# Attention and gated feed-forward on one core: softmax totals on VectorE, layer-norm sums on ScalarE, and a new order

## Chip, core and metric

The kernel runs on one core of one Trainium2 chip. The metric is the device time of one execution in microseconds (us). The engines are TensorE (PE, matmuls; PEld are its weight loads), VectorE (DVE), ScalarE (ACT), GpSimd (POOL) and SyncE (SP, which here only starts DMA transfers). Every engine works through its own instruction list in order and waits, where it must, on semaphores of the others.

## What is computed

The input x has 2048 rows of 512 bf16 numbers. It is normalized row by row; the result xn feeds an attention with 32 heads of 16 numbers, in which every row looks at itself and 7 earlier rows at distances 2, 4, ..., 14, and a gated feed-forward of width 1792:

```python
xn = _layernorm(x)                                  # (x - mean) / sqrt(var + 1e-5)
q, k, v = split(xn @ wqkv)                          # 32 heads x 16
logits = einsum("bhsd,bhswd->bhsw", q, kg) * scale  # kg: the 8 keys at s, s-2, ..., s-14
attn = softmax(where(mask, logits, -1e9))
s = einsum("bhsw,bhswd->bhsd", attn, vg) @ wo
h = gelu(xn @ w_gate) * (xn @ w_up)
return x + s * silu(h @ w_down)
```

## The kernel before

The rows are worked on in four blocks of 512 (j = 0 to 3), each of four tiles of 128 rows. In each block:

- **Layer norm** (`layernorm`, L211; `first_tile`, L321). Per tile, DVE takes the statistics (`stats`, L219, and `aggr`, L223: mean and variance into `mv`). In block 0 ACT takes a square root and DVE inverts it and normalizes; PE transposes the result and ACT copies it into xT. In blocks 1 to 3, POOL computes 1/sqrt(variance + eps) for four tiles at once (`power`, L239 to 243: an addition and a power), DVE makes -mean times that (`shift`, L234, tile `nmr`), ACT normalizes (`norm_act`, L256) and four DMA transposes on SP's queue (`cross`, L307) make xT.
- **q, k, v** (`qkv`, L378; in block 0 `qkv_tiles`, L463, tile by tile). PE multiplies, ACT copies out of PSUM to q, k and a staging tile vst. v goes through DRAM: POOL's queue stores vst to vT (L434; block 0 L497) and loads it back in another layout with the rows that the window reaches back to (`v_loads`, L522, four loads per block, L529). In block 0 the first load needs the first store only.
- **Scores** (`scores`, L542). DVE multiplies q by shifted k (L562, in block 0 half of the products in two halves) and adds the four column groups (L578, two levels); PE adds up within each head with a 0/1 matrix (`reduce`, L600, into the PSUM tile L). DVE takes the maximum over the window (`peak`, L617) and subtracts it (`less`, L624), ACT takes exp (L631), PE adds up the 8 weights with an identity matrix (`total`, L635, 8 matmuls into L), DVE inverts (`recip`, L642) and multiplies (`share`, L646).
- **Values** (`values`, L665). DVE multiplies weights by v (L670, 8 products) and adds them as a tree (L678) to o.
- **Feed-forward** (`ffn`, L701). 14 column groups: PE computes gate and up (L712), ACT evaluates gelu (L728) and copies up (L736), DVE multiplies two groups at a time ("geglu", L750) into h. `down` (L757): PE multiplies h by w_down (L773) in four pieces per tile, of 4, 4, 4 and 2 matmuls; a piece needs the geglu products of its groups. ACT takes silu (L788).
- **Output** (`out`, L799). PE projects o with wo (L807, 64 matmuls into four PSUM tiles), ACT copies out (L821), DVE multiplies by the silu and adds x (L832 and L836; in block 3 per tile, L857 and L863), SP stores.

PSUM: pool F has 6 slots for all these products, of which the projection takes four at once; pool L has one.

The order of every engine's list is not written out. Each operation is entered with an engine, a planned duration, what it needs and a priority (`op`, L167); the function `schedule` (L69) plays this plan through once while the program is built and emits the operations in the order in which they would have started. Its planned durations, latencies (`LAT`), DMA constants (L44 and 45), due times per block (`PARAMS`, L50: N for the layer norm, S scores, V values, Q q/k/v, F feed-forward, Y down) and a seeded jitter of priorities decide the order; none of them changes an instruction. The loads at the start (`loads`, L882) are issued by SP one after the other: x of block 0, wq, wk, wv, x of block 1, gate and up weights, x of block 2, w_down, x of block 3, wo (four copies of it).

Of the kernel before, what the change touches and what calls it, by code (L numbers as in the profile page):

```python
# [41 lines left out]
LAT = {"PE": 0.2, "DVE": 0.1, "ACT": 0.13, "POOL": 0.15}  # L42
DEPENDENT = 0.115
DMA_FIXED = 2.3  # L44
DMA_RATE = {"SP": 325e3, "POOL": 180e3}

POOLS = {"F": 6, "L": 1, "q": 2, "k": 2, "pr": 8, "attn": 2, "Ls": 1, "v": 2, "o": 1, "h": 1,
         "xT": 2, "gl": 3, "sil": 1, "s16": 1, "xn": 4, "vst": 4}

PARAMS = dict(  # L50
    ladd=2, ln_act=4, warm=4, slack=1.0, jitter=(1899, 1.0), N=[-18.9, 13.0, 103.0, 122.5],
    S=[43.3, 66.6, 104.1, 114.9], V=[-8.5, 67.0, 115.5, 125.8], Q=[-7.2, 61.3, 75.8, 119.6],
    F=[3.3, 63.6, 104.7, 160.7], Y=[50.2, 87.1, 133.4, 194.0],
)


# [12 lines left out]
def schedule(ops, pools):  # L69
# [26 lines left out]
    while any(ready.values()):  # L96
        best = None
        for e, rs in ready.items():
            if not rs:
                continue  # L100
            ests = []
            for o in rs:
                t = max(clock[e], at[o.name])
                ok = True
                if o.take:
                    p, n = o.take[0][0], len(o.take)
                    ok = len(free[p]) >= n
# [12 lines left out]
        if best is None:  # L120
            raise RuntimeError("stuck: " + str({e: [o.name for o in r][:6] for e, r in ready.items()}))
        t, o = best
        e = o.eng
        ready[e].remove(o)
        for p, b in o.take:
            _, slot[b] = heapq.heappop(free[p])
        o.start = t
        if o.bytes:
            clock[e] = t + o.dur
            wire[e] = max(wire[e], t + o.dur / 2) + o.bytes / DMA_RATE[e]  # L130
            end = wire[e] + DMA_FIXED
            lanes[e][lane[e]] = end
            lane[e] = (lane[e] + 1) % 8
        else:
            if o.table and o.table != table:
                t += TABLE
                table = o.table
            clock[e] = t + o.dur
            end = clock[e] + LAT[e]
        o.done = end if o.bytes else clock[e] + (DEPENDENT if e == "DVE" else 0.0)  # L140
        o.end = end
        order.append(o)
        for b in o.use:
# [15 lines left out]
class Kernel:  # L159
# [51 lines left out]
    def layernorm(self, j):  # L211
        base = self.when("N", j)
        for tt in range(TPB):
# [25 lines left out]
            def power(a, b):  # L239
                nc = self.nc  # L240
                r = self.rstd[:, a:b, 0]
                nc.gpsimd.tensor_scalar(out=r, in0=self.mv[:, a:b, 1], scalar1=EPS, scalar2=None, op0=ALU.add)
                nc.gpsimd.tensor_tensor(out=r, in0=r, in1=self.mhalf[:, 0 : b - a], op=ALU.pow)

            def norm_dve(t=t):
                nc = self.nc
# [29 lines left out]
            if t == 0:  # L276
                self.first_tile()
                continue
            self.op(f"stats{t}", "DVE", 0.69, [f"ld_x{t if j == 0 else j}_{j}"] + {1: ["aggr0"], 2: ["copy1"]}.get(t, []),
                    stats, prio=prio, slack=(0.0, 0.5, 3.0, 3.0)[j])  # L280
            self.op(f"aggr{t}", "DVE", 0.16, [f"stats{t}"], aggr, prio=prio)
            on_act = t >= self.par["ln_act"]
            if j == 0:
                self.op(f"root{t}", "ACT", 0.25, [f"aggr{t}"], root, prio=prio, table="sqrt")
                self.op(f"rstd{t}", "DVE", 0.1, [f"root{t}"], inverse, prio=prio)
                if on_act:
                    self.op(f"shift{t}", "DVE", 0.1, [f"rstd{t}"], lambda f=shift, t=t: f(t, t + 1), prio=prio)
                ready = f"shift{t}" if on_act else f"rstd{t}"
            else:
                a, b = j * TPB, (j + 1) * TPB  # L290
                if tt == 0:
                    self.op(f"rstd{j}_", "POOL", 1.4, [f"aggr{i}" for i in range(a, b)],
                            lambda f=power, a=a, b=b: f(a, b), prio=prio)
                    self.op(f"shift{j}_", "DVE", 0.1, [f"rstd{j}_"], lambda f=shift, a=a, b=b: f(a, b), prio=prio)
                ready = f"shift{j}_"
            if on_act:
                self.op(f"norm{t}", "ACT", 0.75, [ready], norm_act, take=[("xn", f"xn{t}")],
                        use=[f"xn{t}"], prio=prio)
# [243 lines left out]
    def scores(self, j):  # L542
# [87 lines left out]
            at = self.new(f"at{j}", [P, W, P], BF16, "attn")  # L630
            self.nc.scalar.activation(out=at[:], in_=self.t[f"Ls{j}"][:], func=AF.Exp)  # L631

        def total(j=j):
            for w in range(W):
                self.nc.tensor.matmul(  # L635
                    self.t[f"L{j}"][:, 0, 0:P], lhsT=self.ident[:], rhs=self.t[f"at{j}"][:, w, :],
                    start=(w == 0), stop=(w == W - 1),
                )

        def recip(j=j):  # L640
            with self.nc.allow_low_precision(reason="the weights that it scales are bf16"):
                self.nc.vector.reciprocal(out=self.rs[:, j % 2, :], in_=self.t[f"L{j}"][:, 0, 0:P])  # L642

        def share(j=j):
            at = self.t[f"at{j}"]
# [6 lines left out]
        if j == 0:  # L652
# [3 lines left out]
                use=[f"L{j}", f"Ls{j}"], prio=hot)  # L656
        self.op(f"expo{j}", "ACT", 0.95, [f"less{j}"], expo, take=[("attn", f"at{j}")],
                use=[f"Ls{j}", f"at{j}"], prio=-10.0, table="exp")
        self.op(f"total{j}", "PE", W * MM128, [f"expo{j}"], total, use=[f"at{j}", f"L{j}"], prio=-100.0,
                slack=self.par["slack"])  # L660
        self.op(f"recip{j}", "DVE", 0.95, [f"total{j}"], recip, use=[f"L{j}"], prio=hot)
        self.op(f"share{j}", "DVE", 0.6, [f"recip{j}"], share, use=[f"at{j}"], prio=hot)


# [217 lines left out]
    def loads(self, src):  # L882
# [33 lines left out]
        half = NF // 2 * P  # L916
        kb = 1024
        xt = [(f"ld_x{t}_0", lambda t=t: x_tile(t), 128 * kb) for t in range(TPB)]
        x0 = [("ld_x0_0a", lambda: x_tile(0, 0, D // 2), 32 * kb),
              ("ld_x0_0b", lambda: x_tile(0, D // 2, D, "scalar"), 32 * kb),  # L920
              ("ld_x1_0", lambda: x_tile(1), 192 * kb)]
# [27 lines left out]
def kernel(  # L949
# [33 lines left out]
    k.mhalf = cpool.tile([P, TPB], F32, name="mhalf")  # L983
    k.nmr = cpool.tile([P, NT, 1], F32, name="nmr")
    k.peak = cpool.tile([P, 2, P], F32, name="peak")
    k.rs = cpool.tile([P, 2, P], BF16, name="rs")
    k.ident = cpool.tile([P, P], BF16, name="ident")
    k.ind = cpool.tile([P, H], BF16, name="ind")
# [58 lines left out]
```

## Time and profile before

| what | value |
|---|---|
| time, median of 3 runs | 219.7 us (219.17 to 220.0) |
| time of the profiled execution | 219.26 us |
| its span | 217.3 us |
| last matmul ends | 213.87 us |
| DVE waits for ACT at the last block's output | 5.4 us, once |
| ACT waits for PE at silu (L788) | 21.5 us in 11 waits |
| ACT table loads | 17, of 1.283 us each |
| DMA: v loads (L529), median to landing | 3.8 us; the longest 15.2 us |
| DMA: wo, four copies, median to landing | 16.4 us |

How to read it: the profile shows one execution. Busy times of an engine are the times of its instructions; matmuls are pipelined, so that their durations overlap and the distance from one start to the next tells the pace. The timeline gives start, length and, in brackets, how long the engine was idle before and who ended that. A group line gives the source line, the engine, the operation, its tiles and shapes, the count, then busy us and mean ns of one, then idle time ahead of it. On ACT and DVE an independent instruction starts some 0.1 us before the one ahead of it has ended by the record, so spacing is shorter than length: whole products on DVE are 1.22 us long and 1.135 us apart.

### The profile page before, as it was taken

To read this page: it belongs to the slowest core of one execution; us is meant where nothing else is said; L and a number is where in the kernel's file an instruction comes from. 1 tells how busy PE (TensorE), PEld (TensorE's weight loads), DVE (VectorE), ACT (ScalarE), POOL (GpSimd) and SP (SyncE) were. 2 spreads that over 40 slices of the span, in tenths; PEclk is the share of its full clock that TensorE was granted. 3 is DMA by queue.
4 is the path that set the end of the run, shared out by engine and by line. 5 is a ranking of instruction groups with operands and counts; after the bars stand their busy time and mean duration, and the time that the engine had idled before them with its cause. 6 is when DMAs were issued, how large, how long until landed. Compare 5 with 4: busy or idle time off the path is not lost.

```text
span 217.3 us, 3417 instructions
## 1 busy us (share of the span) xinstructions
PE 209.9 (97%) x1346; PEld 103.1 (47%) x1366; DVE 191.3 (88%) x229; ACT 145.2 (67%) x238; POOL 27.0 (12%) x59
## 2 busy tenths in 40 slices
PE   7999998999999999999999999999999999999993
PEld 2996443444544444454444434544444454444452
DVE  4685999999999997899999969599999999999433
ACT  3687984898987477797624757976732795866151
POOL 5025220220001114002320000001150000000000
PEclk9999999999999999999999999999999999999999
DMA  5999999994000118000490000200123000011002
GB/s 165 363 384 371 306 313 195 187 128 75 0 0 3 48 48 206 0 0 24 112 166 2 0 5 0 97 2 0 53 81 75 0 0 3 0 37 62 0 24 72
DMA packets 18671, 19.59 MB, mean 90 GB/s; under 512 B 7632, under 2 KB 17504, under 8 KB 18528
## 3 DMA queue, kind: packets, MB, share of 16 engines
q1 hardware_dynamic: 16688, 14.88, 26.4%
q0 software_dynamic: 1824, 4.44, 8.1%
q8 instruction: 10, 0.16, 0.3%
q10 hardware_dynamic: 144, 0.07, 0.1%
q14 instruction: 5, 0.04, 0.1%
HBM read 13.60 MB, written 4.21 MB: 82 GB/s over the span
## 4 chain that ended last, share of the span: by engine, by line
PE 70%; DVE 22%; DMA 4%; issue 1%; POOL 1%; ACT 0%; DVEq 0%; POOLq 0%
PE y_ps L773 17%; PE u_ps L712 16%; PE g_ps L712 16%; PE qkv_ps L392 10%; DVE prod L562 7%; PE s_ps L807 7%; DVE prod L578 6%; DVE pv L670 3%; DMA vT_dram<-vst 3%; PE qkv_ps L473 2%; DVE hT L750 2%; DVE pv L678 2%; DMA x_sb<-in_A_x_dram 1%; PE L_ps L600 1%; PE L_ps L635 1%
## 5 line engine op out<-in xcount | busy, mean ns | idle before, releaser
L712 PE MATMUL g_ps<-xnT,wg_sb 128*128 128x512 bf16 x219 | 55.3, 379 | 0.3
L712 PE MATMUL u_ps<-xnT,wu_sb 128*128 128x512 bf16 x219 | 54.8, 379 | 0.2
L773 PE MATMUL y_ps<-wd_sb,hT 128*128 128x512 bf16 (+2 forms) x233 | 49.1, 366 | 0.4 <-issue 0.2
L562 DVE TENSOR_TENSOR prod<-q_sb,k_sb 128x2048 bf16<-128x2048 bf16 (+1 forms) x36 | 38.5, 1101 | 1.6 <-ACT k_sb L489 1.0
L736 ACT ACTIVATE hT<-u_ps 128x512 bf16<-128x512 f32 x56 | 32.9, 600 | 9.5 <-PE u_ps L712 8.7
L728 ACT ACTIVATE gl<-g_ps 128x512 bf16<-128x512 f32 x56 | 33.2, 604 | 7.8 <-PE g_ps L712 7.6
L670 DVE TENSOR_TENSOR pv<-attn,v_arr 128x2048 bf16<-128x2048 bf16 x32 | 38.1, 1220 | 0.1
L773 PEld LDWEIGHTS <-hT 128*128 128x128 bf16 x238 | 22.9, 98 | 25.7 <-issue 0.8
L712 PEld LDWEIGHTS <-wg_sb 128*128 128x128 bf16 x224 | 21.8, 98 | 26.3 <-issue 0.4
L712 PEld LDWEIGHTS <-wu_sb 128*128 128x128 bf16 x224 | 21.5, 98 | 26.4 <-issue 1.5
L678 DVE TENSOR_TENSOR pv<-pv 128x2048 bf16<-128x2048 bf16 x24 | 29.2, 1220 | 0.1
L578 DVE TENSOR_TENSOR prod<-prod 128x2048 bf16<-128x2048 bf16 x24 | 29.1, 1218 | 0.1
L788 ACT ACTIVATE sil<-y_ps 128x512 bf16<-128x512 f32 (+2 forms) x17 | 9.6, 573 | 21.6 <-PE y_ps L773 21.5
L750 DVE TENSOR_TENSOR hT<-hT,gl 128x1024 bf16<-128x1024 bf16 x28 | 19.1, 687 | 2.6 <-ACT hT L736 2.3
L434 POOL DMA_DIRECT2D vT_dram<-vst x12 | 6.7, 559 | 96.2 <-ACT vst L414 96.0
L821 ACT ACTIVATE s<-s_ps 128x512 bf16<-128x512 f32 x16 | 8.9, 602 | 14.4 <-PE s_ps L807 14.4
L807 PE MATMUL s_ps<-wo_sb,o_sb 32*128 32x512 bf16 x256 | 14.5, 375 | 0.0
L529 POOL DMA_DIRECT2D v_arr<-vT_dram x16 | 10.5, 661 | 16.4 <-DMA vT_dram<-vst 12.0
L392 PE MATMUL qkv_ps<-xnT,wk_sb 128*128 128x512 bf16 x46 | 11.9, 380 | 0.1
L392 PE MATMUL qkv_ps<-xnT,wv_sb 128*128 128x512 bf16 x48 | 11.8, 379 | 0.0
L392 PE MATMUL qkv_ps<-xnT,wq_sb 128*128 128x512 bf16 x45 | 11.5, 379 | 0.0
L256 ACT ACTIVATE xn<-x_sb,nmr,rstd 128x512 bf16<-128x512 bf16 x12 | 9.5, 815 | 2.2 <-DVE nmr L234 1.1
(77 smaller groups left out, 177.4 us busy)
## 6 DMA issues: line engine op xcount, KB each, us to landing
v_arr<-vT_dram POOLq DMA_DIRECT2D x16, 142.0 KB, 3.8
vT_dram<-vst POOLq DMA_DIRECT2D x16, 128.0 KB, 2.1
wo_sb<-in_A_wo_dram SPq DMA_DIRECT2D x4, 512.0 KB, 16.4
wg_sb<-in_B_w_gate_dram SPq DMA_DIRECT2D x2, 896.0 KB, 11.0
wu_sb<-in_B_w_up_dram SPq DMA_DIRECT2D x2, 896.0 KB, 13.1
wd_sb<-in_B_w_down_dram SPq DMA_DIRECT2D x1, 1792.0 KB, 19.7
x_sb<-in_A_x_dram SPq DMA_DIRECT2D x3, 512.0 KB, 15.4
out_dram<-s SPq DMA_DIRECT2D x3, 512.0 KB, 3.0
```

Of the source, the lines that this page charges most:

```text
L392: self.nc.tensor.matmul(ps[:], lhsT=self.w_qkv(which, dk, c), rhs=self.t[f"xT{j}"][:, dk, :], start=(dk == 0), stop=(dk == NC - 1),)
L529: self.nc.gpsimd.dma_start(out=self.t[f"v{j}"][H * tq : H * (tq + 1), :, :], in_=self.vT.rearrange("(h d) s -> h d s", d=DH)[:, :, a : a + ...
L562: nc.vector.tensor_tensor(out=self.t[f"pr{j}_{w2}_{c}"][:, :, a:b], in0=self.t[f"q{j}"][:, c, a:b].unsqueeze(1).to_broadcast([P, 4, b - a] ...
L578: self.nc.vector.tensor_tensor(out=pa[:], in0=pa[:], in1=pb[:], op=ALU.add)
L670: self.nc.vector.tensor_tensor(out=pv[:], in0=self.t[f"at{j}"][:, w, :].unsqueeze(1).to_broadcast([P, DH, P]), in1=self.t[f"v{j}"][:, :, 2 ...
L678: self.nc.vector.tensor_tensor(out=out[:], in0=pa[:], in1=pb[:], op=ALU.add)
L712: nc.tensor.matmul(ps[:], lhsT=w[:, dk, fc * P : (fc + 1) * P], rhs=self.t[f"xT{j}"][:, dk, :], start=(dk == 0), stop=(dk == NC - 1),)
L728: self.nc.scalar.activation(out=self.t[f"gl{j}_{pair}"][:, fc % 2, :], in_=self.t[f"ps_g{j}_{fc}"][:], func=AF.Gelu_apprx_tanh,)
L736: self.nc.scalar.activation(out=self.t[f"h{j}"][:, fc, :], in_=self.t[f"ps_u{j}_{fc}"][:], func=AF.Copy)
L750: self.nc.vector.tensor_tensor(out=h, in0=h, in1=self.t[f"gl{j}_{pair}"][:], op=ALU.mult)
L773: nc.tensor.matmul(self.t["ps_" + key][:, 0 : n1 - n0], lhsT=self.t[f"h{j}"][:, fc, tt * P : (tt + 1) * P], rhs=self.wd_sb[:, fc, n0:n1], ...
L807: nc.tensor.matmul(self.t[f"ps_s{j}_{tq}"][:], lhsT=self.t[f"o{j}"][r, d, :], rhs=self.wo_sb[r, d, :], start=(d == 0), stop=(d == DH - 1),)
```

## The change

Three things, and an order that the plan makes anew from them:

1. The totals of the softmax weights are added up on DVE, 8 weights to 4, to 2, to 1, in an fp32 tile `tot` in SBUF, in place of 8 matmuls per block; the reciprocal reads that tile in place of PSUM.
2. In blocks 1 to 3 ACT takes the layer-norm sums with its accumulator: one pass over the tile scaled by -1/512 gives the negative mean, a second one (the square, with that mean as bias) the sum of squared deviations. The full outputs of both go to a scratch tile `junk`. POOL scales the sum by 1/512, adds eps, takes the power and also multiplies the negative mean by it (what DVE's `shift` did).
3. The plan gives a DMA on POOL's queue 3.5 us more to land when it starts before 42 us, and counts other sizes for the first x loads. Due times, slack and jitter seed are others.

```diff
+DMA_CROWDED = 3.5
+LOADED = 42.0
...
-    ladd=2, ln_act=4, warm=4, slack=1.0, jitter=(1899, 1.0), N=[-18.9, 13.0, 103.0, 122.5],
-    S=[43.3, 66.6, 104.1, 114.9], V=[-8.5, 67.0, 115.5, 125.8], Q=[-7.2, 61.3, 75.8, 119.6],
-    F=[3.3, 63.6, 104.7, 160.7], Y=[50.2, 87.1, 133.4, 194.0],
+    ladd=2, ln_act=4, warm=4, slack=0.43, jitter=(4125, 1.0), N=[-7.6, 3.9, 71.2, 106.4],
+    S=[59.8, 41.3, 100.0, 71.3], V=[4.5, 66.8, 111.5, 104.5], Q=[-0.7, 60.2, 73.9, 128.3],
+    F=[10.2, 64.4, 112.5, 164.8], Y=[33.1, 91.5, 146.3, 187.2],
...
-            end = wire[e] + DMA_FIXED
+            end = wire[e] + DMA_FIXED + (DMA_CROWDED if e == "POOL" and t < LOADED else 0.0)
...
-                nc.gpsimd.tensor_scalar(out=r, in0=self.mv[:, a:b, 1], scalar1=EPS, scalar2=None, op0=ALU.add)
+                nc.gpsimd.tensor_scalar(
+                    out=r, in0=self.mv[:, a:b, 1], scalar1=1.0 / D, scalar2=EPS, op0=ALU.mult, op1=ALU.add
+                )
                 nc.gpsimd.tensor_tensor(out=r, in0=r, in1=self.mhalf[:, 0 : b - a], op=ALU.pow)
+                nc.gpsimd.tensor_tensor(out=self.nmr[:, a:b, 0], in0=self.mv[:, a:b, 0], in1=r, op=ALU.mult)
...
+            if j:
+
+                def mean(t=t):
+                    self.nc.scalar.activation(
+                        out=self.junk[:], in_=self.x_sb[:, t, :], func=AF.Identity, scale=-1.0 / D,
+                        accum_out=self.mv[:, t, 0:1],
+                    )
+
+                def square(t=t):
+                    self.nc.scalar.activation(
+                        out=self.junk[:], in_=self.x_sb[:, t, :], func=AF.Square, bias=self.mv[:, t, 0:1],
+                        accum_out=self.mv[:, t, 1:2],
+                    )
+
+                self.op(f"mean{t}", "ACT", 0.65, [f"ld_x{j}_{j}"], mean, prio=prio, slack=(0.0, 0.5, 3.0, 3.0)[j])
+                self.op(f"aggr{t}", "ACT", 0.65, [f"mean{t}"], square, prio=prio)
+            else:
+                self.op(f"stats{t}", "DVE", 0.61, [f"ld_x{t}_0"] + {1: ["aggr0"], 2: ["copy1"]}.get(t, []),
+                        stats, prio=prio)
+                self.op(f"aggr{t}", "DVE", 0.16, [f"stats{t}"], aggr, prio=prio)
...
-                    self.op(f"shift{j}_", "DVE", 0.1, [f"rstd{j}_"], lambda f=shift, a=a, b=b: f(a, b), prio=prio)
-                ready = f"shift{j}_"
+                ready = f"rstd{j}_"
...
-        def total(j=j):
-            for w in range(W):
-                self.nc.tensor.matmul(
-                    self.t[f"L{j}"][:, 0, 0:P], lhsT=self.ident[:], rhs=self.t[f"at{j}"][:, w, :],
-                    start=(w == 0), stop=(w == W - 1),
-                )
+        def total(i, j=j):
+            half = W >> (i + 1)
+            t = self.tot
+            src = t if i else self.t[f"at{j}"]
+            self.nc.vector.tensor_tensor(
+                out=t[:, 0:half, :], in0=src[:, 0:half, :], in1=src[:, half : 2 * half, :], op=ALU.add
+            )
...
-                self.nc.vector.reciprocal(out=self.rs[:, j % 2, :], in_=self.t[f"L{j}"][:, 0, 0:P])
+                self.nc.vector.reciprocal(out=self.rs[:, j % 2, :], in_=self.tot[:, 0, :])
...
-        self.op(f"total{j}", "PE", W * MM128, [f"expo{j}"], total, use=[f"at{j}", f"L{j}"], prio=-100.0,
-                slack=self.par["slack"])
-        self.op(f"recip{j}", "DVE", 0.95, [f"total{j}"], recip, use=[f"L{j}"], prio=hot)
+        last = f"expo{j}"
+        for i in range(3):
+            last = self.op(f"total{j}_{i}", "DVE", (0.6, 0.33, 0.2)[i], [last], lambda i=i, f=total: f(i),
+                           use=[f"at{j}"], prio=hot)
+        self.op(f"recip{j}", "DVE", 0.95, [last], recip, prio=hot)
...
+    k.junk = cpool.tile([P, D], BF16, name="junk")
+    k.tot = cpool.tile([P, W // 2, P], F32, name="tot")
```

What the new order moves, read from the built programs: on POOL the rstd of block 1 and its two companions stand behind the four v stores of block 0 and the first v load, and ahead of the other three v loads (before, they stood behind two stores and the first load; two stores and three loads followed). On ACT the 24 new passes stand between the copies and gelus of block 0 and the first half of block 1, all ahead of the copies of the output projection of block 0. On PE the projection of block 2 moves behind the feed-forward of block 3, the reduction of block 3 into the down products of block 2, and the projections of blocks 0, 1 and 3 stand a few matmul groups earlier. SP issues the same transfers in the same order. ACT loads its tables 17 times, as before.

More of the change, by code (lines that the diff above doesn't have):

```diff
@@ L278, in layernorm @@
                 continue
[L279 to L282, printed above, removed]
+            if j:
[15 more added lines that the diff above has]
+                self.op(f"aggr{t}", "DVE", 0.16, [f"stats{t}"], aggr, prio=prio)
+            on_act = j > 0 or t >= self.par["ln_act"]
             if j == 0:
@@ L291, in layernorm @@
                 if tt == 0:
-                    self.op(f"rstd{j}_", "POOL", 1.4, [f"aggr{i}" for i in range(a, b)],
+                    self.op(f"rstd{j}_", "POOL", 2.1, [f"aggr{i}" for i in range(a, b)],
                             lambda f=power, a=a, b=b: f(a, b), prio=prio)
-                    self.op(f"shift{j}_", "DVE", 0.1, [f"rstd{j}_"], lambda f=shift, a=a, b=b: f(a, b), prio=prio)
-                ready = f"shift{j}_"
+                ready = f"rstd{j}_"
             if on_act:
@@ L918, in loads @@
         xt = [(f"ld_x{t}_0", lambda t=t: x_tile(t), 128 * kb) for t in range(TPB)]
-        x0 = [("ld_x0_0a", lambda: x_tile(0, 0, D // 2), 32 * kb),
-              ("ld_x0_0b", lambda: x_tile(0, D // 2, D, "scalar"), 32 * kb),
-              ("ld_x1_0", lambda: x_tile(1), 192 * kb)]
+        x0 = [("ld_x0_0a", lambda: x_tile(0, 0, D // 2), kb),
+              ("ld_x0_0b", lambda: x_tile(0, D // 2, D, "scalar"), kb),
+              xt[1]]
         wt = [(f"ld_w{'qkv'[i]}", lambda i=i: w_qkv(i), 512 * kb) for i in range(3)]
```

## The prediction

> **What bounds the kernel now.** I read the page first, its busy times and its slices, then the waits of PE, then PE's timeline.
>
> ```profile
> PE 209.9 (97%) x1346; PEld 103.1 (47%) x1366; DVE 191.3 (88%) x229; ACT 145.2 (67%) x238; POOL 27.0 (12%) x59
> ...
> PE   7999998999999999999999999999999999999993
> ...
> PEclk9999999999999999999999999999999999999999
> DMA  5999999994000118000490000200123000011002
> ```
>
> PE is full from the second slice to the last but one, at full clock; the DMA engines are full until 49 us. A matmul of 512 columns lasts 379 ns in the groups, but four start 0.865 us apart, so PE delivers one in 0.216 us. Waits of PE:
>
> ```profile
> PE warm_ps L184 <- DVE eps L995: 1.2, 1, 1.2
> PE L_ps L600 <- DVE prod L578: 0.9, 1, 0.9
> ```
>
> Behind the start PE waits once, in block 0's reduction (L600). Adding up PE's list at its pace puts the next matmul at 35.31; it starts at 36.37, so this wait costs 1.06 us. PE's last matmul ends at 213.87, 3.43 us before the span ends. So time is PE's work, plus that wait, plus ends that the change leaves alone.
>
> **The change, part by part.** The sums go against the profiled execution, 219.26 us (span 217.3). The median is 219.7, 0.44 above; a shift found for one holds for the other.
>
> *Totals off PE.* Two of the four places in PE's timeline (start, length):
>
> ```profile
> 44.15 0.61 PE L635 MATMUL L_ps<-attn,ident 128*128 128x128 bf16 x8
> 44.60 10.96 PE L773 MATMUL y_ps<-wd_sb,hT 128*128 128x512 bf16 x49
> ```
>
> From start to next start they take 0.45, 0.44, 0.44 and 0.45: **1.78 us** less for PE, on the path.
>
> *VectorE.* Groups, with mean ns:
>
> ```profile
> L219 DVE BATCH_NORM_STATS2 stats<-x_sb 128x6 f32<-128x512 bf16 x15 | 9.6, 673 | 1.0 <-DMA x_sb<-in_A_x_dram 1.0
> L223 DVE BATCH_NORM_AGGREGATE mv<-stats 128x2 f32<-128x6 f32 x15 | 2.3, 174 | 0.0
> L624 DVE TENSOR_TENSOR Ls<-L_ps,peak 128x1024 f32<-128x1024 f32 x4 | 4.9, 1220 | 0.0
> L256 ACT ACTIVATE xn<-x_sb,nmr,rstd 128x512 bf16<-128x512 bf16 x12 | 9.5, 815 | 2.2 <-DVE nmr L234 1.1
> ```
>
> Removed: 12 x (0.673 + 0.174) + 3 x 0.157 (nmr, L234) = 10.6. Added: per block three fp32 additions of 512, 256 and 128 elements. No such row exists; upper bound by a line through fp32 rows (128 elements 0.269, 1024 elements 1.220): 0.68 + 0.41 + 0.27 = 1.35; lower by bf16 rows of 512, 320 and 192 (0.425, 0.326, 0.258): 1.0. I take 1.35, as the output is fp32: 5.4 in all. DVE loses 5 us of work. Ahead of block 0's reduction go the stats pass at 34.2 (0.60 to the next start) and the 2.58 us in which the nmr operation of block 1 waited for POOL (18.3 to 20.9).
>
> *Block 0's wait.* Walking DVE's new list: the last k copy of block 0 ends on ACT at 16.85 (in place of 16.35; three of the new passes stand between the copies: 12.76 + 4 x 0.48 + 3 x 0.65 + 0.2 of waiting and completion). Behind it stand four half products and three geglu products, spaced 0.603, and ten whole products and additions, spaced 1.135: 16.85 + 7 x 0.603 + 10 x 1.135 + 0.2 = 32.6. PE asks for the last of them at 34.2. The wait goes: **1.06 us**.
>
> What is late next, with PE never stopping? I laid PE's new order at its pace, and DVE's beside it:
>
> - output projection (L807) of block 0: PE at 66.4; its input is ready 21.2 behind the start of the first value product (18 operations x 1.135, one geglu, 0.2).
> - reductions of blocks 1, 2, 3: ready 0.7, 1.5 and 0.9 ahead of PE (83.1, 125.5, 159.4).
> - projections of blocks 1, 2, 3: ready 0.8, 0.9 and 3.6 ahead of PE (121.8, 194.2, 200.9).
>
> So DVE is on time, but never by much. All hangs on when the first value product can start.
>
> *The first value product* needs the shares and v. Shares: the reduction ends at 34.65, mask, peak, geglu and less (0.25, 1.25, 0.6, 1.14) at 37.9. ACT comes to exp at 38.3 (from 14.46: ten of the new passes at 0.65, four normalizations at 0.72, 26 copies and gelus at 0.48, a table load, 0.6 of small pieces), table load 1.28, exp 1.06: 40.7. Additions with a geglu between: 42.7; reciprocal and share with their spacings 1.06 and 0.73: 44.55. The projection of block 0 could then start at 65.75, with 0.7 to spare: v may come until 45.25. *v* is the trouble. POOL before (start, length):
>
> ```profile
> 18.75 0.67 POOL L529 DMA_DIRECT2D v_arr<-vT_dram  x1 [4.81 <-DMA vT_dram<-vst]
> 19.45 0.25 POOL L242 TENSOR_SCALAR rstd<-mv 128x4 f32<-128x4 f32 x1
> 19.78 1.04 POOL L243 TENSOR_TENSOR rstd<-rstd,mhalf 128x4 f32<-128x4 f32 x1
> 20.80 1.60 POOL L497 DMA_DIRECT2D vT_dram<-vst  x2
> 22.39 0.67 POOL L529 DMA_DIRECT2D v_arr<-vT_dram  x1
> 28.23 1.42 POOL L529 DMA_DIRECT2D v_arr<-vT_dram  x2 [5.17 <-DMA vT_dram<-vst]
> ```
>
> Now block 1's rstd, with its new multiplication, stands ahead of three of the four v loads and waits for ACT's last square of that block, 27.4. Its operations: 1.35 as before, and the multiplication between 0.24 (L242) and 1.04 (L243), say 0.35 (a plain operation). The three loads are issued from 29.2 to 31.3, not at 22.4, 28.2 and 28.9. The old ones took 7.2, 11.1 and 15.2 to land, the last at 44.15, while the wo load filled the engines until about 46. Bounds for the new last one: 44.2 (the engines drain at the old time) and 50 (29.2 + 11.1 for the first, 4.85 more for each next, as between the old two). I take 46.0, near the old drain: v is one transfer more behind the same SP traffic, but SP got that room earlier. The first value product starts at 46.1, and the projection of block 0 is **0.85 us** late; the later meetings keep their order. No other stage waits for v: blocks 1 to 3 issue theirs over 10 us ahead.
>
> Of sharing the engines, the Trainium skill ("DMA: Bandwidth & Descriptors", arbitration) says that each engine alternates between queues packet by packet. The 15.2 us beside a full SP queue agree; it would let v finish no later than SP's backlog, 46.
>
> *ScalarE* gets 24 passes (mean, square). Row: the normalization from the same tile, 0.815 long, two follow 0.70 to 0.82 apart; copies out of PSUM 0.48 apart. An accumulating pass is not in the trace. Bounds 0.48 and 0.82 (I know nothing that makes it cheaper than a copy); I take the middle, 0.65: 15.6 us more, ACT 145 to 161. A square waits for its mean; queued behind it on ACT are the copies that empty PE's slots, so it matters only where the two stand together (twice, 0.1 each). By the skill ("ScalarE: Activation LUTs", what a table load costs) a pass would be 0.52 with immediate operands and 0.61 with a pointer, next to the copies' and normalizations' rows; then ACT would be sooner by about 1.6 us over block 0's stage, and v alone would decide.
>
> At 0.65 ACT runs without a pause from 14.5 to 66, catching up with PE there: the copy of k1's last tile ends at 65.8, and the projection of block 0 needs its PSUM slot (six in F, four taken at once, L812) at 66.4. Margin 0.6. From there on ACT's list holds what it held before, shifted.
>
> *At no cost:* the POOL multiplication (ACT reaches the first normalization of block 1 at 30.2, rstd is there at 29.2; 1 us of cover); the transposes on SP (xT1 landed by 50, PE asks at 54.3; the ring is in the same order, behind wo); table loads (17 before and after); planned sizes of the x loads (the plan alone). The tail has the same list: last y, silu, gate, add, store.
>
> **Sum:** -1.78 - 1.06 + 0.85 = -1.99 in 219.26: 217.3; from the median 217.7. I say **217.5**.
>
> **Rivals.**
>
> 1. *v in time.* Landing by 45.2, as the drain's bound allows: 216.4. For it: no more bytes are moved. Against: three loads issued 2 to 7 us later.
>
> 2. *ScalarE too full.* Pass of c us: about 20 of them stand on a gapless ACT ahead of the projection of block 0, so the slot comes 20 x (c - 0.65) later, less 0.6 of margin. At 0.75: 1.4 late, 217.8; at 0.82, the upper bound: 2.8, **219.2**. It is lost against before from c = 0.82 on, and more than 0.5% slower from 0.88, if accumulating costs above every row. For it: in the walk ACT has no pause in this stage. Against: PSUM copies at 0.48. The skill's rule speaks for it (same page, rules for kernel authors: additions and multiplications on VectorE, not ScalarE).
>
> 3. *v very late.* Landing at 50: first value product at 50.1, the projection of block 0 is 4.85 late: **221.3**, slower. It decides from 49.2 on (4.0 late, 220.4). For it: two loads issued 0.7 apart landed 4.85 apart. Against: wo has drained by 46.
>
> 4. *The change doesn't do it:* the reduction of block 0 still waits, since ACT hands over k later: 218.4. It would need DVE 1.6 late where 3.3 us of waits and stats go from it.
>
> **Chances.** Forecast 0.46 (216.9 to 218.2), v in time 0.17, ScalarE 0.22 (217.8 to 220.5), v very late 0.10, rival 4 0.05. Range: 216.3 to 220.0; it leaves out most of rival 3 and the end of rival 2. About 0.5%, 1.1 us, is what a measurement can tell here. Faster (under 218.2): nearly all of the forecast, v in time, a third of ScalarE: 0.68. Same: half of ScalarE, rival 4, the forecast's end: 0.18. Slower: v very late and the end of ScalarE: 0.14.
>
> **What would show it.** PE's waits without L600 of block 0; no matmuls of the totals; a wait of PE for the projection of block 0, about 0.8 (or ahead of it at y_ps, for the geglu product that is queued behind the first value product on DVE); a DVE wait for DMA ahead of that product, about 1.5; passes of 0.65 apart on ACT; PE's last matmul ending at 211.9. Wrong if ACT's k copies come late (PE waiting for ACT near 66), or if DVE's waits move to geglu products.

## The result, and the profile after

The changed kernel takes 222.1 us (median of six runs, 221.06 to 224.43); the kernel before, run beside it, 219.65 us. The ratio is 1.0108, with a 95% interval of 1.0069 to 1.0148: it is slower, where 217.5 us was forecast, and above the range. Ratios here and below count a kernel's runs within 1.5% of its fastest one, which leaves out the run of 224.43. The profiled execution took 221.36 us, with a span of 219.3 us, 2.0 more than before.

Line numbers are now those of the changed kernel: rstd on POOL is L244, L247 and L248 (`power`), the ACT passes L287 (mean) and L293 (square), the normalization L261, products and their additions L583 and L599, the reduction L621, geglu L774, up L760, y L797, the projection L831, v loads L550.

The page's busy times and clock, and PE's waits (us in total, times, the longest):

```profile
PE 210.1 (96%) x1315; PEld 101.7 (46%) x1334; DVE 187.6 (86%) x214; ACT 158.7 (72%) x286; POOL 34.6 (16%) x62
...
PEclk9999999969999999999999999999999999999999
```

```profile
PE y_ps L797 <- ACT hT L760: 2.1, 1, 2.1
```

The wait at block 0's reduction is gone, as forecast. In its place PE waits once for ACT, ahead of the y product of block 0, and in the slice behind that wait the granted clock is down to 6 tenths. Going back from that wait, ACT is late because of this, in its timeline (start, length, and in brackets the idle time ahead and who ended it):

```profile
34.47 0.81 ACT L261 ACTIVATE xn<-x_sb,nmr,rstd 128x512 bf16<-128x512 bf16 x1 [3.80 <-POOL nmr L248]
```

ACT, which has no time to spare in this stage, stands still for 3.80 us for the rstd of block 1. POOL's timeline shows why:

```profile
28.11 4.93 POOL L244 TENSOR_SCALAR rstd<-mv 128x4 f32<-128x4 f32 x1 [7.36 <-ACT junk L293]
33.12 1.04 POOL L247 TENSOR_TENSOR rstd<-rstd,mhalf 128x4 f32<-128x4 f32 x1
34.24 0.20 POOL L248 TENSOR_TENSOR nmr<-mv,rstd 128x4 f32<-128x4 f32 x1
34.46 2.01 POOL L550 DMA_DIRECT2D v_arr<-vT_dram  x3
```

An operation on four numbers per partition, which took 0.25 us before (L242), is under way for 4.93 us, though ACT's last sum, which it waited for, is there when it starts. DVE at that time:

```profile
26.62 2.35 DVE L583 TENSOR_TENSOR prod<-q_sb,k_sb 128x2048 bf16<-128x2048 bf16 x2
28.89 2.35 DVE L599 TENSOR_TENSOR prod<-prod 128x2048 bf16<-128x2048 bf16 x2
31.16 0.68 DVE L774 TENSOR_TENSOR hT<-hT,gl 128x1024 bf16<-128x1024 bf16 x1
31.77 1.22 DVE L599 TENSOR_TENSOR prod<-prod 128x2048 bf16<-128x2048 bf16 x1
36.29 0.69 DVE L774 TENSOR_TENSOR hT<-hT,gl 128x1024 bf16<-128x1024 bf16 x1 [3.31 <-ACT hT L760]
```

From 17.3 on DVE runs operations on two SBUF tensors without a pause. The last of this run ends at 32.98, and POOL's operation at 33.04.

The clock behind PE's wait, in windows of 2 us: the window and its length, then busy time and count of PE, weight loads, DVE, ACT and POOL, then the granted clock, the DMA share and GB/s:

```profile
44.00:46.00 2.00, 0.51 (x2) 0.19 (x2) 0.98 (x2) 1.98 (x4) 0.00 (x0) 0.94 1.05 70
46.00:48.00 2.00, 2.00 (x6) 0.76 (x5) 1.93 (x5) 1.99 (x3) 0.00 (x0) 0.50 0.89 163
48.00:50.00 2.00, 2.00 (x8) 0.77 (x7) 1.97 (x3) 1.99 (x5) 0.00 (x0) 0.71 0.01 4
```

PE starts 6 and 8 matmuls of 512 columns in 2 us; in the next window it is 11, at a clock of 1.00.

**The balance of the span.** Less: the totals, 1.78, and the wait at L600, 1.06. More: a start 0.46 later (first transpose at 5.61, was 5.15; the second x tile landed later); 0.55 in two places ahead of the wait, where PE's next group starts 0.22 and 0.33 behind its pace (40.35 and 41.54); 2.22 at the wait (45.49, where the pace gives 42.40 + 0.865 = 43.27); and 1.64 by the clock (the y product takes 13.77 us to the next group, at full clock 12.13, as the second probe's kernel shows below). Together +2.03; the span grew by 2.0. In this execution all of the loss lies ahead of 59 us: behind it PE waits for nothing, and the last matmul ends 3.43 us before the end, as before.

### The profile page after: what moved, and what is told of

It is laid out like the page before. It is cut to its first block, busy times and chain, and to the rows that moved or that the text cites. A ratio compares the mean times of both kernels' runs of the same rounds, so it can differ in the third digit from the quotient of the medians.

```text
span 219.3 us, 3393 instructions
## 1 busy us (share of the span) xinstructions
PE 210.1 (96%) x1315; PEld 101.7 (46%) x1334; DVE 187.6 (86%) x214; ACT 158.7 (72%) x286; POOL 34.6 (16%) x62
## 4 chain that ended last, share of the span: by engine, by line
PE 79%; ACT 12%; POOL 3%; issue 2%; DMA 1%; DVE 1%; SPq 0%
PE y_ps L797 23%; PE g_ps L736 17%; PE u_ps L736 16%; PE qkv_ps L413 14%; PE s_ps L831 7%; POOL rstd L244 2%; ACT hT L760 2%; ACT gl L752 2%; PE qkv_ps L494 2%; ACT junk L293 2%; DMA x_sb<-in_A_x_dram 1%; ACT junk L287 1%; ACT xn L261 1%; ACT vst L515 1%; PE L_ps L621 1%
## 5 line engine op out<-in xcount | busy, mean ns | idle before, releaser
L797 PE MATMUL y_ps<-wd_sb,hT 128*128 128x512 bf16 (+2 forms) x232 | 50.9, 375 | 2.6 <-ACT hT L760 2.1
L583 DVE TENSOR_TENSOR prod<-q_sb,k_sb 128x2048 bf16<-128x2048 bf16 (+1 forms) x36 | 38.4, 1098 | 4.0 <-ACT k_sb L510 4.0
L760 ACT ACTIVATE hT<-u_ps 128x512 bf16<-128x512 f32 x56 | 33.0, 601 | 7.1 <-PE u_ps L736 6.8
L797 PEld LDWEIGHTS <-hT 128*128 128x128 bf16 x238 | 23.3, 100 | 29.6 <-issue 5.5
L599 DVE TENSOR_TENSOR prod<-prod 128x2048 bf16<-128x2048 bf16 x24 | 28.7, 1216 | 0.1
L774 DVE TENSOR_TENSOR hT<-hT,gl 128x1024 bf16<-128x1024 bf16 x28 | 19.1, 681 | 6.2 <-ACT hT L760 6.2
L831 PE MATMUL s_ps<-wo_sb,o_sb 32*128 32x512 bf16 x256 | 14.5, 375 | 0.0
L261 ACT ACTIVATE xn<-x_sb,nmr,rstd 128x512 bf16<-128x512 bf16 x12 | 9.5, 808 | 3.9 <-POOL nmr L248 3.8
L413 PE MATMUL qkv_ps<-xnT,wq_sb 128*128 128x512 bf16 x47 | 12.1, 380 | 0.1
L550 POOL DMA_DIRECT2D v_arr<-vT_dram x16 | 10.5, 663 | 7.8 <-DMA vT_dram<-vst 4.3
```

What stands on the lines that cost most here:

```text
L261: nc.scalar.activation(out=xn[:], in_=self.x_sb[:, t, :], func=AF.Identity, scale=self.rstd[:, t, :], bias=self.nmr[:, t, :],)
L413: self.nc.tensor.matmul(ps[:], lhsT=self.w_qkv(which, dk, c), rhs=self.t[f"xT{j}"][:, dk, :], start=(dk == 0), stop=(dk == NC - 1),)
L583: nc.vector.tensor_tensor(out=self.t[f"pr{j}_{w2}_{c}"][:, :, a:b], in0=self.t[f"q{j}"][:, c, a:b].unsqueeze(1).to_broadcast([P, 4, b - a] ...
L599: self.nc.vector.tensor_tensor(out=pa[:], in0=pa[:], in1=pb[:], op=ALU.add)
L760: self.nc.scalar.activation(out=self.t[f"h{j}"][:, fc, :], in_=self.t[f"ps_u{j}_{fc}"][:], func=AF.Copy)
L774: self.nc.vector.tensor_tensor(out=h, in0=h, in1=self.t[f"gl{j}_{pair}"][:], op=ALU.mult)
```

## Experiments

Theory A: a POOL operation that reads SBUF is held off while DVE works on two SBUF tensors at a time, without a pause. Rivals: B, the two-operation form on POOL has to load code at its first use (one queue of instruction loads, q14 on the page, has 6 packets, before 5; the page does not say whose it is); C, ACT is too full in block 0 whatever POOL does.

### A probe at the setup

```diff
+    probe = cpool.tile([P, TPB], F32, name="probe")
+    nc.gpsimd.tensor_scalar(out=probe[:], in0=k.mhalf[:], scalar1=1.0 / D, scalar2=EPS, op0=ALU.mult, op1=ALU.add)
```

> Adds one more two-operation tensor_scalar of 128x4 fp32 on GpSimd at the setup, about 4 us into the span, where VectorE has little to do; nothing else changes. Theory A (GpSimd's operation is held off as long as VectorE runs products of two SBUF tensors without a pause): the added operation takes about 0.25 us, block 1's rstd operation (L244) still takes 4 to 5 us and ends when VectorE's run ends, near 33; ScalarE still waits 3.8 us; time as after, 221 to 222.5. Theory B (the first use of this form on GpSimd has to load code, 4.7 us): the added operation takes about 4.9 us instead, block 1's takes 0.3 to 0.7, ScalarE's wait of 3.8 us is gone, and with it PE's 2.06 us and the slower clock behind: 217 to 217.6.

Measured: 222.77 us (one execution). POOL's timeline:

```profile
4.06 0.20 POOL L1042 TENSOR_SCALAR probe<-mhalf 128x4 f32<-128x4 f32 x1
...
29.49 4.92 POOL L244 TENSOR_SCALAR rstd<-mv 128x4 f32<-128x4 f32 x1 [7.33 <-ACT junk L293]
```

The first use of the form costs 0.20 us, and block 1's operation is as long as in after. B is out. The time is 0.3 us above the band. (The operation comes 1.4 us later than in the profile of after because PE's first 32 matmuls in this execution took 3.39 us, there 1.78; see the last section.)

### A probe in the middle of VectorE's run

The same operation, put into POOL's list behind the first v load (`if o.name == "ldv0_0"` in the loop that emits the order).

> Adds the same two-operation tensor_scalar of 128x4 fp32 on GpSimd right behind the first v load of block 0, near 20.8 us, in the midst of VectorE's run of products from 17.3 to 33.0; its operand is ready from the setup on. Theory A (held off by VectorE's run): the added operation lasts until VectorE's run ends, about 12 us, block 1's rstd follows from 33 on; time as after, 221 to 222.5 or a little more. Theory B (code load at first use): the added operation takes about 5 us and ends near 26; block 1's operation at 28.1 then takes 0.3 to 0.7 and ScalarE has no wait of 3.8 us: 217 to 217.6.

Measured: 224.29 us (one execution).

```profile
20.80 1.31 POOL L1046 TENSOR_SCALAR probe<-mhalf 128x4 f32<-128x4 f32 x1
...
73.49 8.42 POOL L244 TENSOR_SCALAR rstd<-mv 128x4 f32<-128x4 f32 x1
```

The time is above the band, by 1.8 us. Block 1's operation takes 4.93 us again. The probe was held too, but for 1.31 us and not the 12 that I had from A: it came in at the end of an addition, at 22.11, while DVE went on without a gap. So A as I put it was too strong: at some ends of DVE's operations POOL gets in, at others not. The same kernel has a longer hold, 8.42 us, at block 3's rstd, from 73.49 until DVE's run ends at 81.86. In the profile of after that operation took 0.36. PE pays for the long one with 1.44 and 1.72 us of waits at 84.7 and 91.2 (and 0.54 earlier, for k), but had no slow clock this time: the y product took 12.13 us behind the same wait of 2.06.

### The multiplication back on VectorE

```diff
-                nc.gpsimd.tensor_tensor(out=self.nmr[:, a:b, 0], in0=self.mv[:, a:b, 0], in1=r, op=ALU.mult)
+                nc.vector.tensor_tensor(out=self.nmr[:, a:b, 0], in0=self.mv[:, a:b, 0], in1=r, op=ALU.mult)
```

> The multiplication that makes nmr (mean times rstd) goes back from GpSimd to VectorE; in VectorE's list it stands behind the seventh product of block 0's reduction, so VectorE stops there until GpSimd has made rstd, as it stopped at 18.3 in before. Theory A (held off by VectorE's run): VectorE stops near 29.0, GpSimd's two operations then take 0.25 and 1.04 and end near 30.4, ScalarE normalizes at 30.7 without a wait of 3.8 us; VectorE's reduction of block 0 is ready 1.5 us later, near 34.5, which PE meets at 34.3: time 217 to 218. Theory B (code load at first use): GpSimd's first operation still takes 4.9 us from 28.1, VectorE stops until 34.2, the reduction of block 0 is 5 us late for PE: 223 to 226.

Measured: 219.18 us, ratio to before 0.997 (0.9935 to 1.0004); span of the profiled run 217.0.

```profile
27.89 0.91 POOL L244 TENSOR_SCALAR rstd<-mv 128x4 f32<-128x4 f32 x1 [7.35 <-ACT junk L293]
```

DVE now stops behind a product that ends at 28.75, waiting for POOL, and POOL's operation ends at 28.80. ACT has no wait there, PE neither its 2.06 us nor the slow clock. Against after this is 3 us faster, but still 1.2 us above the band that I gave. PE's waits say where it went:

```profile
PE s_ps L831 <- DVE o_sb L702: 1.2, 1, 1.2
PE L_ps L621 <- DVE prod L599: 1.0, 1, 1.0
```

Both come from the edit itself, which makes DVE wait for POOL in blocks 2 and 3 too. The second is block 1's reduction, where DVE stood still for 1.20 us at block 3's rstd. The first is the projection of block 0, in whose products and additions DVE stood still for block 2's rstd:

```profile
50.65 0.16 DVE L248 TENSOR_TENSOR nmr<-mv,rstd 128x4 f32<-128x4 f32 x1 [1.31 <-POOL rstd L247]
```

DVE also waited 0.57 us for v ahead of its first value product, but that alone would not have made PE wait (see "Why the prediction was wrong").

### Block 1's statistics back on VectorE (e4_block1)

```diff
+    def block1():
+        for t in range(TPB, 2 * TPB):
+            nc.vector.bn_stats(out=k.stats[:, t, :], in_=k.x_sb[:, t, :])
+            nc.vector.bn_aggr(out=k.mv[:, t, :], in_=k.stats[:, t, :])
+        r = k.rstd[:, TPB : 2 * TPB, 0]
+        nc.gpsimd.tensor_scalar(out=r, in0=k.mv[:, TPB : 2 * TPB, 1], scalar1=EPS, scalar2=None, op0=ALU.add)
+        nc.gpsimd.tensor_tensor(out=r, in0=r, in1=k.mhalf[:], op=ALU.pow)
...
     for o in order:
+        if o.name == "prod0_0_0":
+            block1()
+        if o.name == "ladd0_0_0_0":
+            shift1()          # nmr, the operation of before
+        if o.name not in gone:  # mean, square and rstd of block 1
             o.emit()
```

> After, with the layer-norm sums of block 1 alone put back on VectorE, in the 3.7 us in which it waits for ScalarE's k copies (13.6 to 17.3), and block 1's rstd on GpSimd right behind them, ahead of VectorE's run of products; nmr by one VectorE operation behind the half products, as in before. Blocks 2 and 3 stay on ScalarE. Theory A (GpSimd's operation was held off by VectorE's run, and all of the loss in block 0 follows from that): rstd is there near 18, ScalarE's wait of 3.8 us, PE's wait of 2.06 us and the slow clock behind it go, and 8 passes of 0.66 leave the full ScalarE: after's 221.4 less 2.1, 0.7 of small gaps and 1.7 of clock: 216.5 to 217.5, with 1 to 3 us more in runs where block 3's rstd operation is held. Rival C (ScalarE is too full in block 0 whatever GpSimd does, rival 2 of the prediction): no wait of ScalarE for GpSimd, yet PE still waits near 43 or 66 by 1 us or more: 218.5 to 220.

Measured: 220.26 us, ratio to before 1.0057 (1.0025 to 1.0089); span 218.0.

```profile
69.26 8.42 POOL L244 TENSOR_SCALAR rstd<-mv 128x4 f32<-128x4 f32 x1
```

```profile
PE L_ps L621 <- DVE prod L599: 1.7, 1, 1.7
PE qkv_ps L413 <- ACT gl L752: 1.4, 1, 1.4
```

In block 0 all went as A says: no wait of PE between 6 and 80 us. This kernel has eight ACT passes less in block 0, so by itself it does not rule out C; but with the passes kept and only the hold gone (the multiplication on VectorE above, the statistics passes below) PE has no wait for ACT ahead of 80 us either. So C falls. The time is above 217.5, within the 1 to 3 us that the band's last clause allows: block 3's rstd is held for 8.42 us, ACT waits 4.6 us for it, and PE 1.44 and 1.73 us at 80.5 and 87.0. 218.0 less these 3.17 would be 214.8.

### The totals alone

Before, with only the additions on DVE in place of the matmuls of the totals (the part of the diff from `def total` on, and the tile `tot`), ordered by before's parameters.

> The one part alone: before, with the softmax totals by three fp32 additions on VectorE; layer norm as before (the planner orders the work anew by before's parameters). By theory A the totals are not at fault: PE gets 1.78 us of matmuls less, VectorE 5.5 us more; block 0's reduction still makes PE wait about 1 us, and the value products of block 0 come about 1 us later, for which PE may wait up to 1.5 us at the output projection: 217.5 to 219. If the totals are what costs (VectorE too full), it is slower than before: 220 to 223.

Measured: 219.06 us, ratio to before 0.9984 (0.9958 to 1.001): no difference. PE gains its 1.78 us and gives back 1.45 in one wait at 26.1 us (for ACT's gelu; ACT waits 3.22 us for block 1's nmr in the new order). The wait at block 0's reduction, which I had expected to stay, is gone too, but the span ends 4.7 us behind the last matmul, in before 3.43. So totals on DVE are not what made the changed kernel slower. (The profiled execution, span 219.2, is one with the slow first matmuls of the last section; the median is not.)

### The sums alone

Before, with only the layer-norm part of the diff (ACT's two passes, POOL's three operations), ordered by before's parameters.

> The other part alone: before, with the layer-norm sums of blocks 1 to 3 on ScalarE and the nmr multiplication on GpSimd; totals stay on PE (ordered anew by before's parameters). Theory A: block 1's rstd operations on GpSimd fall into VectorE's run of products and are held for several of them (3 us or more in the first operation), ScalarE waits for them, and PE behind ScalarE: 221 to 225. If GpSimd is not held, ScalarE goes through and the wait at block 0's reduction is gone: 218 to 219.

Measured: 222.45 and 222.60 us in the two runs that the ratio counts, 1.0128 (1.0079 to 1.0177): slower, in the band of A. Two more runs took 228.27 and 228.37, at a mean granted clock of 0.992; neither has a profile that says why.

```profile
29.24 1.94 POOL L242 TENSOR_SCALAR rstd<-mv 128x4 f32<-128x4 f32 x1
```

This operation, for less than the 3 us that I had expected, and the power behind it (2.03 us) are held; ACT waits 3.27 us for the third, and PE 1.83 us for exp. The wait at block 0's reduction is gone here too.

### A busy VectorE with one SBUF input

```diff
+        if o.name == "prod0_1_3":
+            for t in range(3):
+                nc.vector.bn_stats(out=k.probe[:, t, :], in_=k.x_sb[:, t, :])
```

> After, with three statistics passes of 128x512 bf16 (0.67 us each, one tensor read, result unused) put into VectorE's run of products where block 1's rstd operation waits, from about 29.0 to 30.9. VectorE is then still busy without a pause, but for 1.9 us not with operations that read two SBUF tensors. If it is such operations that hold GpSimd off: the rstd operation ends within 0.1 us of the first pass's start, at 29.0, its power 1.04 later, the multiplication near 30.4, and ScalarE's wait of 3.8 us is gone; the reduction of block 0 is ready 1.9 us later and PE waits there about 0.6: 217 to 218.5. If any busy VectorE holds it: the operation ends near 35, ScalarE waits 5 to 6 us: 223 to 226.

Measured: 220.53 us (one execution). DVE, then POOL:

```profile
26.18 2.36 DVE L583 TENSOR_TENSOR prod<-q_sb,k_sb 128x2048 bf16<-128x2048 bf16 x2
28.45 1.88 DVE L1046 BATCH_NORM_STATS2 probe<-x_sb 128x6 f32<-128x512 bf16 x3
```

```profile
27.67 0.92 POOL L244 TENSOR_SCALAR rstd<-mv 128x4 f32<-128x4 f32 x1 [7.30 <-ACT junk L293]
28.68 1.04 POOL L247 TENSOR_TENSOR rstd<-rstd,mhalf 128x4 f32<-128x4 f32 x1
```

POOL's operation ends at 28.59, 0.05 behind the product, and its power and its multiplication (0.20 us) run at their own pace beside DVE's passes with one input, though DVE has no pause. So it isn't a busy DVE that holds POOL, but DVE with two SBUF inputs. The power carries this: beside additions with two inputs, at the same place, it took 1.91 us (next section). The first operation came in here at the end of a product, as it did in the next kernel without any statistics passes. The time misses the band: block 0 is free of waits, but block 3's rstd is held for 8.42 us again and costs the same 1.44 and 1.73.

### Writes and reads

Four memsets and four two-operation tensor_scalars, all of 128x4 fp32, at the place of the second probe.

> After, with eight small operations more on GpSimd behind the first v load of block 0, near 20.8, in VectorE's run of products: four memsets of 128x4 fp32 (they only write), then four two-operation tensor_scalars of 128x4 fp32 (they read and write). If it is GpSimd's reading that is held off: the memsets take about 0.1 us each and are done by 21.3, and each tensor_scalar ends about 0.05 us behind the end of one of VectorE's operations, whichever: 1 to several of those operations apart, up to VectorE's idle time at 33. If writing is held off too, the first memset already lasts to the end of an operation of VectorE, 22.1 or later. Which end of an operation lets GpSimd in is what neither theory says. Time no help here: 221 to 225, as the v loads wait behind.

Measured: 221.35 us (one execution). The four memsets and one of the four tensor_scalars, and DVE at that time:

```profile
20.71 0.22 POOL L1046 MEMSET probe<- 128x4 f32 x4
...
21.99 1.07 POOL L1048 TENSOR_SCALAR probe<-mhalf 128x4 f32<-128x4 f32 x1
```

```profile
21.79 1.22 DVE L583 TENSOR_TENSOR prod<-q_sb,k_sb 128x2048 bf16<-128x2048 bf16 x1
```

The memsets, which only write, pass beside DVE's addition (20.66 to 21.88). Each tensor_scalar ends 0.05 us behind the end of a DVE operation (this one at 23.06, the product at 23.01), and the next comes in at the next end. Here even block 1's rstd came in at the first end (0.93 us), at the very change from product to addition at which it was held in after; the power behind it, beside the additions (28.67 to 31.02), took 1.91:

```profile
28.89 1.91 POOL L247 TENSOR_TENSOR rstd<-rstd,mhalf 128x4 f32<-128x4 f32 x1
```

Why the same place lets POOL in here and not there stays open.

### Both holds out of the way

The kernel with block 1's statistics on DVE, and besides:

```diff
+    late = {"rstd3_": None, **{f"{n}{t}": None for n in ("norm", "copy") for t in range(3 * TPB, NT)}}
+    after = {"ldv1_3": ["rstd3_"], "up1_12": ["norm12"], "gelu1_13": ["norm13"], "up1_13": ["norm14"],
+             "copy12": ["norm15"], "silu1_0_0": ["copy12", "copy13", "copy14", "copy15"]}
     for o in order:
...
+        if o.name in late:
+            late[o.name] = o.emit
+        elif o.name not in gone:
             o.emit()
+        for n in after.get(o.name, ()):
+            late.pop(n)()
```

> The version with block 1's statistics on VectorE (as in e4_block1), and block 3's rstd on GpSimd moved from 69.3, in VectorE's run of products, to behind the last v load of block 1, about 85, where VectorE takes block 1's peak a little later (from 89.1); ScalarE's four normalizations of block 3 move behind it, to about 100 to 115. Theory A: what e4_block1 still lost, PE's waits of 1.44 and 1.73 at 80 and 87, followed from the 8.42 us hold of block 3's rstd operation; both go, and 218.0 of span less 3.2 gives 214.8 to 215.5, time 216.8 to 217.6, ratio to before 0.985 to 0.992. If they had another cause (VectorE late for block 1's reduction, ScalarE too full), PE still waits 1 us or more near 80 or 87: 218.5 or more.

Measured: **216.63 us**, ratio to before 0.9875 (0.9843 to 0.9907): faster than both kernels; the ratio is in the band, the time 0.2 us below it.

```profile
80.54 0.54 POOL L244 TENSOR_SCALAR rstd<-mv 128x4 f32<-128x4 f32 x1
```

```profile
PE warm_ps L186 <- DVE eps L1021: 1.2, 1, 1.2
PE y_ps L797 <- issue: 0.3, 2, 0.2
```

Behind the start PE waits for no engine any more. The operation came at 80.5, not at 85 as I had it, and was held for 0.3 us only; but ACT now asks for it only about 20 us later, so that a hold would cost nothing.

### The changed kernel once more

> The changed kernel itself again, beside the others on the same chip, for its spread. If the length of the holds on GpSimd (0.36 or 8.42 us for block 3's operation, by the traces so far) sets the kernel's time, its runs fall into groups 1 to 3 us apart, as the first six did (221.1 to 221.4, 222.9, 224.4), all above before: median 221 to 224.5.

Measured: 223.8 us (220.75 to 224.41), ratio 1.0159 (1.0103 to 1.0215). The profiled one has block 1's operation at 4.93 us again, the same wait of 2.06 and the clock at 0.51 behind it; block 3's takes 0.36. The runs lie 1.4 to 5.0 us above before's median and up to 3.7 apart. Over this set and the first, the six runs with a mean granted clock of 0.992 took 220.75 to 223.16 us, the six with 0.999 or 1.000 took 223.62 to 224.43: the longest runs are those without the slow clock, so the balance above is that of one kind of execution. The second probe's kernel, with the hold of 8.42 us and a clock of 0.999, took 224.29. That the length of block 3's hold is what parts the runs fits this, but is not shown, as only one run of each set has a profile.

## Why the prediction was wrong

**The step that failed** is "Its operations: 1.35 as before, and the multiplication ... say 0.35 (a plain operation)", and with it "At no cost: the POOL multiplication (... 1 us of cover)". Block 1's rstd was forecast to take 1.7 us and took 6.3 (28.11 to 34.44). With it fell "At 0.65 ACT runs without a pause from 14.5 to 66": ACT stood still for 3.80 us, and PE waited for ACT ahead of the y product of block 0, which cost 2.22 us, a wait that the prediction does not have. I took the durations from rows, but not the state of the neighbour in which these rows were measured. In the trace of before the three groups of POOL run at 19.5 in DVE's wait for them, at 39.0 beside the peak (which reads PSUM) and at 44.8 beside the reciprocal (one input), here the last two (the first stands in the prediction):

```profile
39.00 0.23 POOL L242 TENSOR_SCALAR rstd<-mv 128x4 f32<-128x4 f32 x1 [9.35 <-DVE mv L223]
...
44.78 0.23 POOL L242 TENSOR_SCALAR rstd<-mv 128x4 f32<-128x4 f32 x1 [4.42 <-DVE mv L223]
```

None of these additions ran beside an operation with two SBUF inputs. The powers behind them reached 0.35 and 0.22 us into a geglu that started later, and took 1.04 all the same. So that trace held no price for a POOL operation that comes in behind such a DVE operation. Bounds from both sides were due for all three operations; I gave them to the multiplication only, and only for its own length. The wait of DVE for POOL of 2.58 us, which I booked as a gain, was also what had kept DVE silent for POOL.

The Trainium skill has the rule that I passed over ("SBUF — State Buffer", "Who interferes with whom"): a VectorE instruction with two SBUF inputs contends with a GpSimd instruction that reads SBUF, not with one that only writes, and a VectorE instruction with one SBUF input does not contend. The runs here agree on all three: tensor_scalars beside DVE's products and additions took 0.35 to 8.42 us (0.20 alone), memsets 0.12, and the power beside statistics passes 1.04, its own pace. They differ in the measure: by the same page of the Trainium skill ("SBUF: two separate sides") the loser is blocked for the whole instruction of the other, and 4.93 us spans the ends of four DVE operations.

Point by point:

- *Totals off PE, 1.78:* right.
- *Block 0's wait, 1.06:* right. DVE's last addition ended at 32.98 (forecast 32.6, plus 0.46 of later start), PE came at 34.28.
- *Additions, 1.35 per block:* right: 0.69, 0.42 and 0.28, 1.39.
- *An ACT pass, 0.65 (rival 2):* right. The mean takes 0.61 from start to start, the square 0.71, each with its reading of the accumulator of 0.2 us, overlapped by half; they lie 0.09 and 0.10 above the lower prices that the prediction gives beside its own, by about the part of that reading that shows. ACT was through at 30.67, which is the forecast 30.2 plus the later start. That ACT is too full: only after the 3.80 us of standing still. With those gone (the multiplication on VectorE, 8 passes more than in the fast version), PE had no wait for ACT at all.
- *v late, 0.85:* could not show in after, where the shares were later still. In the run with the multiplication on VectorE the three loads were issued from 29.89, where the forecast had 29.2, and the first value product started at 45.25 after a wait for v of 0.57. The forecast had 46.1 and allowed v until 45.25. With its 21.2 us to the projection, the input would have been there at 66.45; PE, which waited 1.19 until 67.90, asked at 66.71. So there v cost nothing, the term was too large by all of its 0.85, and PE's wait came from DVE's 1.31 us at block 2's rstd.
- *Rivals:* v in time (1) fits that run. Rivals 2, 3 and 4 are not what happened in after. What did, POOL held off by DVE, was not among them.
- *What would show it:* the list named DVE and ACT, and no sign on POOL; its own timeline, four lines, shows the cause.

What is settled: the hold (two placements of the same operation, reads against writes, one input against two), its path to PE's waits by way of ACT, and that with both holds out of the way and block 1's statistics on DVE the change is 1.25% faster than before. Not settled: which end of a DVE operation lets POOL in, what the slow clock depends on, and what parts the changed kernel's runs.

## What to carry to other kernels

A duration read from a row holds for what the neighbours did then: before a small operation is moved on GpSimd, look at what VectorE runs at the new place, and if that is a gapless run of operations on two SBUF tensors, take the rest of that run as the upper bound of its price, and keep it off the path of whoever waits for the result. A wait that the change removes may have been what made room for another engine. Operations with slack (here a normalization needed 20 us later) should be asked for late, not as soon as their inputs allow.

## What the runs showed of the hardware

- POOL's tensor_scalars of 128x4 that meet a DVE operation with two SBUF inputs end 0.05 to 0.1 us behind the end of such an operation, not always of the first: the same operation took 0.20 us alone and 0.35 to 8.42 beside a run of them. The power, 1.04 us by itself, then took 1.9 and ended 0.9 behind (73.98 to 75.87 in after, DVE's addition ending at 74.98). DVE itself was not slowed: its products last 1.22 us while POOL's power runs beside them.
- A wait of PE of 2.06 us was followed by a granted clock of 0.50 for some 3.4 us, which cost 1.64 us (profiles of after, of its repeat and of the kernel with the probe at the setup), or was not (1.00 in the kernel with the probe in the run). The Trainium skill ("TensorE: Matmul & The Clock Gate", "What's actually happening") has the clock go to half after a window of about 3.4 us of idling, with windows that run freely. The length agrees; 2.06 us of waiting is less than its window. PE was busy for 1.94 of the 4 us from 42 to 46 in after, and just as long where the clock stayed at 1.00.
- The first 32 matmuls of 128 columns (q of block 0) take 3.4 us in three of the twelve profiled executions and 1.8 to 2.0 in the others, also of the same kernel, at a recorded clock of 1.00:

```profile
6.60 3.60 PE L494 MATMUL qkv_ps<-xnT,wq_sb 128*128 128x128 bf16 x32
```

  This line is of the repeat of after; the profile of after has 1.95 in its place. In the two executions of the changed kernel's order in which it was so (this one and the probe at the setup), block 1's rstd came 1.8 and 1.4 us later than in after. The runs of before (219.0 to 221.3) spread by about as much; that this is why is not shown.
- The accumulator of ACT is read by an instruction of its own, 0.19 to 0.27 us, of which a copy behind it hides about half (13.73 to 13.82 from start to start in after); another pass behind it hides nothing (50.56 to 50.78).
